# One-tile fp32 jobs for two experts after five units, a two-tile fp32 job after seven, and a written order through the ninth unit

## The chip, the core and the metric

One core of a Trainium2 chip runs the whole program. The metric is device time in microseconds, as the median of three runs. The engines are PE (TensorE, matmuls; its weight loads are PEld), DVE (VectorE), ACT (ScalarE), POOL (GpSimd) and SP (SyncE, which here only issues transfers).

## The reference

A gated scan over 4 sequences of 3648 steps with 256 channels, and then a mixture of 16 experts in 4 groups of 4, of which each token takes one.

```python
sig = 1.0 / (1.0 + np.exp(-f_logit))
f = lower_bound + (1.0 - lower_bound) * sig
for t in range(S):
    h = f[:, t] * h + (1.0 - f[:, t]) * x[:, t]
    y[:, t] = h
# x = y as 14592 tokens of 256
g_idx = argmax(x @ w_group); g_w = softmax(x @ w_group)[g_idx]
# for the tokens of group g
e_idx = argmax(xg @ w_expert[g]); e_w = softmax(xg @ w_expert[g])[e_idx]
h = np.maximum(xg @ w1[g, e], 0.0)      # 256 -> 1024
out = g_w * e_w * (h @ w2[g, e])        # 1024 -> 256
```

## The kernel before

Phase 1 goes through the tokens in 29 units of 512 (`UNIT`). For each unit a transfer brings gate and input (tile `zt`, 1 MB; p1_load, SP for units under 9, then ACT's queue, two units ahead). ACT makes tanh and affine (p1_tanh, p1_affine; together p1_ta), DVE the gated product and the scan of both halves of the channels (p1_gate, p1_tb), PE the routing logits (p1_router, p1_logits) and the transposes back to token rows (p1_back, tile `rows`). Every one or two units (GROUPS) a routing step on DVE and PE works out the place of each token in its expert's list (`posi`), and POOL scatters the rows, 128 at a time, into the lists `xs` in DRAM (s7).

Phase 2 is the experts. Each expert has an early job, kind A: EARLY gives for expert e the unit count after which the list is cut (first number), and how many tiles of 128 rows are taken from below the cut (second). close_early works out the place (`posA`), early_rows has SP read the rows (`xr`), and early_blanks writes blank rows ahead of the list, for a list that is still shorter. Sixteen jobs of kind B, longest first, then take what is left of each list; CAPS is the row count for which each of them is built, and a loop at the end would take what exceeds a cap.

A job has four pieces of weights, 512 KB each (job_weights), then its rows transposed (job_xt: `xh`, `xl`), a first layer (m1_step, banks of 512 columns, `hh`, `hl`) and a second one (m2_step, 8 matmuls of 256 columns and a row scale `o`, then POOL's scatter to the output). Ordinary jobs split weights, rows and hidden values into an fp16 high and a bf16 low part (job_split: a cast to `wh` on ACT, a subtraction to `wl` on DVE) and use three matmuls for a product. The first RAW jobs take fp32 as it is, with one matmul that runs in several passes, and `xh`, `xl`, `wh`, `wl`, `hh`, `hl` are then just halves of the channels.

Order: up to unit 8 the program gives PE, DVE and ACT their order as written (manual_schedule; p1_thunks with `u <= cut + 1`). Afterwards the steps of phase 1 are dealt out between the steps of the jobs at a rate (`due`, bg_step), and a scheduler may move an instruction of one engine ahead of others. Job 0 starts when `marks["begun"]` is reached. SP issues in the order written throughout:

```python
for u, n in EARLY_FETCH:
    while u not in last_load:
        bg_pop()
    fetch_to(n)
bg_to(first)
start_macro(0)
```

Of the kernel before, what the change touches and what calls it, by code (L numbers as in the profile page):

```python
# [24 lines left out]
CAPS = [848, 748, 724, 592, 588, 560, 528, 488, 464, 460, 448, 420, 392, 296, 168, 112]  # L25
# [3 lines left out]
EARLY_FETCH = [(5, 4), (8, 8)]  # L29
STG_BUFS = 8  # L30
RAW = 2
# [10 lines left out]
def gated_scan_moe(ctx: ExitStack, tc, zx, lower, wroute, wexp, out, S):  # L42
# [234 lines left out]
    def route_thunks(G, T, fast=False):  # L277
# [64 lines left out]
        def s7(t0, t1):  # L342
            for t in range(t0, t1):
# [43 lines left out]
    def p1_thunks(us, groups):  # L387
# [28 lines left out]
        cut = EARLY[0][0]  # L416
# [13 lines left out]
        for u in us + [us[-1] + 1]:  # L430
            seq = []
            if u <= cut + 1:
                put(lambda u=u: (p1_load(u + AHEAD - 1), early_blanks(u + 4)))
                ending = u - 1 in ends and u <= cut
# [7 lines left out]
                put(lambda u=u: p1_tb(u, 0))  # L442
                if ending:
# [5 lines left out]
                    if u > 1 and member[u - 2] == member[u - 1]:  # L449
                        put(lambda u=u: p1_back(u - 2, 0))  # L450
                        put(lambda u=u: p1_back(u - 2, 1))
# [4 lines left out]
                    put(lambda u=u: p1_back(u - 1, 0))  # L456
                    put(lambda u=u: p1_back(u - 1, 1))
# [5 lines left out]
                elif u > cut:  # L463
                    put(lambda u=u: p1_back(u - 1, 0))
                    put(lambda u=u: p1_back(u - 1, 1))
                if u == cut:
                    put(lambda u=u: close_early(u))
                    f = lambda u=u: early_rows(u)
                    f.mark = u
                    put(f)  # L470
                f = lambda u=u: p1_tb(u, 1)
                if u == cut + 1:
                    f.mark = "begun"
                put(f)
# [14 lines left out]
            for t in seq:  # L489
                put(t)  # L490
                slot += 1
                for _ in range(2 if u <= EARLY[0][0] else 1):
# [9 lines left out]
            if u - 1 in ends:  # L502
# [10 lines left out]
                if u in cuts and u > cut:  # L513
# [36 lines left out]

    def early_rows(u):
        for mac in macros:
# [5 lines left out]
    early_loads = []  # L558

# [551 lines left out]
```

## Time and profile before

| | |
|---|---|
| median of 3 runs (lowest, highest) | 815.78 us (814.15, 817.62) |
| profiled execution: time, span | 819.72 us, 818.0 us |
| PE busy | 732.8 us, 90% of the span |
| DVE, ACT, POOL busy | 525.2, 453.8, 284.3 us |
| PE share of the chain that ended last | 73% |
| mean DMA rate | 190 GB/s |

Busy time is the time in which an engine had an instruction in work. A row of the timeline has the start, the duration, the engine (a q behind it marks the issue of a transfer), line, operation, tiles written and read, and in brackets how long the engine had been idle and what released it. PE records an fp32 matmul twice.

### The profile page before, as it was taken

What the parts mean: (1) busy time and instruction counts of PE and PEld (TensorE: products, weight loads), DVE (VectorE), ACT (ScalarE), POOL (GpSimd) and SP (SyncE); (2) the same over time, 40 slices, a digit from 0 to 9 for tenths busy, and PEclk for the clock granted to TensorE, in tenths of its full rate; (3) what the DMA queues carried; (4) which work ended last, traced back from release to release, by engine and by line L of the source; (5) the groups of instructions that cost most, each with busy time, mean ns of one, the idle gap of its engine ahead of it and who ended that gap; (6) DMA issues with size and microseconds to landing.
All of it is one profiled execution on the core that took longest, in us unless ns stands there. A gap on an engine that the chain in (4) does not pass through costs nothing.

```text
span 818.0 us, 20715 instructions
## 1 busy us (share of the span) xinstructions
PE 732.8 (90%) x8048; PEld 640.5 (78%) x8048; DVE 525.2 (64%) x1040; ACT 453.8 (55%) x818; POOL 284.3 (35%) x272
## 2 busy tenths in 40 slices
PE   2644888999999898779999999999999999999996
PEld 1423667889788687569898898998988989889995
DVE  6755889899889776266555535545545656555650
ACT  6445487877677755235454445544544655556641
POOL 3662264477646352541112222212222222132222
PEclk9999989999999899999999999999999999999998
DMA  7997989999999645329553552543643555555400
GB/s 264 333 314 230 348 232 385 325 338 330 344 247 348 214 131 175 110 76 284 125 127 113 141 123 82 143 114 109 165 119 111 144 152 160 164 163 156 119 28 23
DMA packets 97156, 155.57 MB, mean 190 GB/s; under 512 B 52448, under 2 KB 64765, under 8 KB 93728
## 3 DMA queue, kind: packets, MB, share of 16 engines
q1 hardware_dynamic: 82080, 103.73, 43.9%
q0 software_dynamic: 11424, 30.02, 10.7%
q10 hardware_dynamic: 3552, 20.48, 6.8%
q8 instruction: 63, 1.03, 0.5%
q14 instruction: 37, 0.30, 0.1%
HBM read 112.69 MB, written 42.02 MB: 189 GB/s over the span
## 4 chain that ended last, share of the span: by engine, by line
PE 73%; issue 6%; DVE 5%; DMA 4%; ACT 1%; POOL 1%; POOLq 0%; DVEq 0%; SPq 0%; ACTq 0%
PE ps_m L894 35%; PE ps_m L871 8%; PE ps_m L873 8%; PE ps_m L872 7%; PE ps_p L872 3%; PE ps_p L871 3%; PE ps_p L873 3%; DMA zt<-in_zx_dram 3%; DVE wl L775 2%; PE ps_p L249 2%; PE ps_p L818 1%; PE ps_p L263 1%; PE ps_m L888 1%; PE ps_m L849 1%; POOL out_dram L907 1%
## 5 line engine op out<-in xcount | busy, mean ns | idle before, releaser
L894 PE MATMUL ps_m<-wl,hh 128*128 128x256 bf16 (+4 forms) x1288 | 259.9, 252 | 7.0 <-issue 6.9
L894 PE MATMUL ps_m<-wh,hl 128*128 128x256 f16 (+4 forms) x1288 | 259.6, 252 | 4.0 <-issue 4.0
L894 PE MATMUL ps_m<-wh,hh 128*128 128x256 f16 (+4 forms) x1288 | 259.9, 253 | 2.0 <-issue 1.7
L894 PEld LDWEIGHTS <-hh 128*128 128x128 f16 (+3 forms) x2576 | 191.0, 100 | 31.8 <-issue 11.7
L871 PE MATMUL ps_m<-xh,wh 128*128 128x256 f16 (+7 forms) x750 | 187.8, 260 | 7.6 <-issue 4.8
L872 PE MATMUL ps_m<-xl,wh 128*128 128x256 bf16 (+7 forms) x750 | 187.9, 260 | 2.0 <-DVE xl L828 1.4
L873 PE MATMUL ps_m<-xh,wl 128*128 128x256 f16 (+7 forms) x750 | 187.8, 260 | 1.2 <-issue 1.2
L775 DVE TENSOR_TENSOR wl<-st,wh 128x1024 bf16<-128x1024 f32 x120 | 144.9, 1218 | 64.5 <-ACT wh L774 62.9
L344 POOL DMA_INDIRECT xs<-rows,posi x114 | 133.4, 1170 | 135.1 <-DVE rows L326 49.3
L877 DVE SCALAR_TENSOR_TENSOR hl<-ps_m,hh 128x512 bf16<-128x512 f32 (+7 forms) x168 | 112.0, 669 | 92.4 <-issue 49.5
L907 POOL DMA_INDIRECT out_dram<-o,info x75 | 82.1, 1095 | 254.7 <-ACT o L906 210.5
L876 ACT ACTIVATE hh<-ps_m 128x512 f16<-128x512 f32 (+7 forms) x168 | 98.7, 589 | 91.1 <-PE ps_m L873 61.7
L774 ACT CAST wh<-st 128x1024 f16<-128x1024 f32 x120 | 124.3, 1049 | 11.7 <-PE ps_m L894 7.7
L894 PEld LDWEIGHTS <-hl 128*128 128x128 bf16 (+4 forms) x1288 | 102.1, 100 | 20.0 <-issue 9.9
L872 PEld LDWEIGHTS <-wh 128*128 128x128 f16 x1056 | 103.6, 98 | 17.8 <-issue 10.2
L873 PEld LDWEIGHTS <-wl 128*128 128x128 bf16 x1056 | 103.5, 98 | 12.5 <-issue 5.2
L871 PEld LDWEIGHTS <-wh 128*128 128x128 f16 x1056 | 103.8, 98 | 11.6 <-issue 3.6
L907 POOL DMA_INDIRECT out_dram<-o,meta x55 | 64.3, 1169 | 137.0 <-ACT o L906 120.6
L906 ACT ACTIVATE o<-ps_m,info 128x256 f32<-128x256 f32 (+4 forms) x75 | 33.1, 441 | 95.9 <-PE ps_m L894 86.4
L872 PE MATMUL ps_p<-xl,wh 128*128 128x256 bf16 (+13 forms) x306 | 73.5, 252 | 1.8 <-issue 1.8
L873 PE MATMUL ps_p<-xh,wl 128*128 128x256 f16 (+13 forms) x306 | 73.5, 252 | 0.5 <-issue 0.4
L871 PE MATMUL ps_p<-xh,wh 128*128 128x256 f16 (+13 forms) x306 | 73.7, 252 | 0.0
(165 smaller groups left out, 806.4 us busy)
## 6 DMA issues: line engine op xcount, KB each, us to landing
st<-in_wexp_dram SPq DMA_DIRECT2D x120, 512.0 KB
zt<-in_zx_dram ACTq DMA_DIRECT2D x19, 1024.0 KB
zt<-in_zx_dram SPq DMA_DIRECT2D x7, 1024.0 KB
xr<-xs SPq DMA_DIRECT2D x25, 258.0 KB
xs<-blank SPq DMA_DIRECT2D x22, 258.0 KB
wh<-in_wexp_dram SPq DMA_DIRECT2D x8, 256.0 KB
wl<-in_wexp_dram SPq DMA_DIRECT2D x8, 256.0 KB
xs<-rows,posi POOLq DMA_INDIRECT x114
```

The costliest lines, as they stand in the source:

```text
L249: nc.tensor.transpose(out=bp[:, (j - j0) * D + k * P:(j - j0) * D + (k + 1) * P], in_=h[:, k, j * P:(j + 1) * P], identity=ident)
L344: sc = nc.gpsimd.indirect_dma_start(out=xs_v[G["t0"] + t][:, :], out_offset=bass.IndirectOffsetOnAxis(ap=R["posi"][:, t:t + 1], axis=0), i ...
L774: nc.scalar.copy(j.wh[i], j.st[i])
L775: nc.vector.tensor_tensor(out=j.wl[i], in0=j.st[i], in1=j.wh[i], op=ALU.subtract)
L871: nc.tensor.matmul(po, w1_at(j.wh, k, c), xh[:, k], start=(k == 0), stop=False)
L872: nc.tensor.matmul(po, w1_at(j.wh, k, c), xl[:, k], start=False, stop=False)
L873: nc.tensor.matmul(po, w1_at(j.wl, k, c), xh[:, k], start=False, stop=(k == KD - 1))
L876: nc.scalar.activation(hi, pv, AF.Relu)
L877: nc.vector.scalar_tensor_tensor(out=j.hl[ch][:, cs[0]:cs[-1] + 1, 0:w], in0=pv, scalar=0.0, in1=hi, op0=ALU.max, op1=ALU.subtract)
L894: nc.tensor.matmul(pm[i * q:i * q + n, 0:dw], h[ch][:, c, ts], w2_at(w, c)[:, i * dw:(i + 1) * dw], start=(c == 0 and s == 0), stop=(c == ...
L906: nc.scalar.activation(o[s, 0:dw], pm[s, 0:dw], AF.Copy, scale=lt.bitcast(F32)[s, r, 1:2])
L907: nc.gpsimd.indirect_dma_start(out=out_v[out_n[0]].rearrange("n (g d) -> (n g) d", g=g), out_offset=bass.IndirectOffsetOnAxis(ap=lt[s, r, ...
```

## The change

EARLY: experts 0 and 1 are cut after five units with one tile (before: seven, two tiles); expert 2 after seven (before nine), expert 4 after nine (before eleven). CAPS grow to match. RAW goes from 2 to 3. The written order runs through unit 9 (FAST), and jobs 0 and 1 stand in it as parts that p1_thunks puts at the ninth unit (PLAN, first_parts, wave); their second layer is cut in two (raw2). Their rows are asked for at unit 8, those of job 2 at unit 9 (ROWS_AT). A read of early rows no longer waits for scatters of units behind its cut, nor a tail blank for any scatter. Weights are fetched up to 6 or 8 pieces ahead, but at most two at a time.

```diff
-EARLY = [(7, 2), (7, 2), (9, 2), (9, 2), (11, 2), (11, 2), (13, 3), (15, 3),
+EARLY = [(5, 1), (5, 1), (7, 2), (9, 2), (9, 2), (11, 2), (13, 3), (15, 3),
-CAPS = [848, 748, 724, 592, 588, 560, 528, 488, ...
+CAPS = [976, 812, 748, 616, 592, 588, 548, 488, ...
-EARLY_FETCH = [(5, 4), (8, 8)]
+EARLY_FETCH = [(5, 4), (8, 8), (-5, 12)]
+FAST = 9
+PLAN = [9, 9]
+ROWS_AT = {5: 8, 7: 9}
-RAW = 2
+RAW = 3
...
+                scatters.append(((G["t0"] + t) // (UNIT // P), sc.ins))
...
+        def wave(u, n):
+            while parts and n and parts[0][0] <= u:
+                put(parts.pop(0)[1])
+                n -= 1
...
-            if u <= cut + 1:
-                put(lambda u=u: (p1_load(u + AHEAD - 1), early_blanks(u + 4)))
-                ending = u - 1 in ends and u <= cut
+            if u <= FAST:
+                put(lambda u=u: (p1_load(u + AHEAD - 1), [early_blanks(v) for v in range(u + 4 if u else 0, u + 5)]))
+                for m in [m for m, v in ROWS_AT.items() if u == v]:
+                    f = lambda m=m: early_rows(m)
+                    f.mark = m
+                    put(f)
+                ending = u - 1 in ends
...
                 put(lambda u=u: p1_tb(u, 0))
+                wave(u, 1)
...
                     put(f4)
+                    wave(u, 1)
...
                     for f in s7s:
                         put(f)
+                    wave(u, 1)
...
+                put(lambda u=u: p1_tb(u, 1))
+                wave(u, 1 if u < FAST else 99)
...
     def tail_blank(s):
...
+        for _, sc in scatters:
+            tc.declare_no_dep(bl.ins, sc, reason="blank rows begin behind a list's last row")
...
                 early_loads.append(ld.ins)
+                for u, sc in scatters:
+                    if u >= EARLY[j.idx][0]:
+                        tc.declare_no_dep(ld.ins, sc, reason="rows scattered behind a cut lie above it")
...
+    def raw2(j, ch, t, cs, pm):
+        b, n, _ = j.parts[ch][t]
+        c0 = b - j.chunks[ch][0]
+        for c in cs:
+            nc.tensor.matmul(pm[0:n, 0:D], j.hh[ch][c // 4][:, c % 4, c0:c0 + n],
+                             (j.wh, j.wl)[c % 4 // 2][2 + c // 4][:, c % 2 * D:(c % 2 + 1) * D],
+                             start=(c == 0), stop=(c == KF - 1))
...
+    def first_parts():
+        out = []
+        for (j,), u in zip(macros, PLAN):
+            half = {}
+
+            def begin(j=j, half=half):
+                half[0] = bank("m2")
+                raw2(j, 0, 0, range(KF // 2), half[0])
+            fs = [lambda j=j: job_xt(j, 0)]
+            fs += [lambda j=j, cs=cs: m1_step(j, 0, cs) for cs in j.cols[0]]
+            fs += [begin, lambda j=j, half=half: m2_step(j, 0, 0, half[0])]
+            out += [(u, f) for f in fs]
+        return out
...
-            fetch_to(piece_index[(id(j), i)] + STG_BUFS)
+            at = piece_index[(id(j), i)]
+            fetch_to(max(at + 1, min(at + (6 if j.raw else STG_BUFS), pptr[0] + 2)))
...
         bg_to(marks["begun"])
-        for t in prep:
+        start_macro(len(PLAN))
+        for t in prep_thunks(macros[len(PLAN)][0]):
             t()
...
+        if mi < len(PLAN):
+            continue
```

What it moves, on two engines. ACT in the stretch in which units 8 and 9 are worked on, before: the tanh of unit 9 (L185), the transfer of unit 11 (L175), the affine of unit 9 (L195), the router copy (L266), the tanh of unit 10, the logits (L275), unit 10's affine between the row copies of unit 7 (L251), and job 0's rows (L824).

```order
L185 ACTIVATE zt<-zt 128x1024
L175 DMA zt<-in_zx_dram 128x2048
L195 ACTIVATE zt<-zt,mid,half 128x512 x2
L266 COPY rs<-ps_p 128x128
L185 ACTIVATE zt<-zt 128x1024
L275 COPY Lg<-ps_p 128x80
L195 ACTIVATE zt<-zt,mid,half 128x512
L251 COPY rows<-ps_p 128x2x256
L253 COPY rows<-tokno 128x4
L195 ACTIVATE zt<-zt,mid,half 128x512
L251 COPY rows<-ps_p 128x2x256
L824 COPY xh<-ps_p 128x256
```

The same place after, from the transfer of unit 11 on (lines are shifted: L178 is the transfer, L188 the tanh, L198 the affine, L856 a raw job's rows, L884 a raw job's hidden values).

```order
L178 DMA zt<-in_zx_dram 128x2048
L269 COPY rs<-ps_p 128x128
L178 DMA zt<-in_zx_dram 128x2048
L278 COPY Lg<-ps_p 128x80
L856 COPY xh<-ps_p 128x128
L856 COPY xl<-ps_p 128x128
L188 ACTIVATE zt<-zt 128x1024
L375 ACTIVATE ex<-ge 128x160
L188 ACTIVATE zt<-zt 128x1024 x2
L198 ACTIVATE zt<-zt,mid,half 128x512 x4
L884 ACTIVATE hh<-ps_m_914 128x4x128
L198 ACTIVATE zt<-zt,mid,half 128x512 x2
```

Job 0's rows now come before the tanh of unit 10, and the tanh of units 10, 11 and 12, the second transfer of the piece being unit 12's, stand ahead of job 0's first hidden values. Further down on ACT after, between job 0 and job 2:

```order
L806 CAST wh_1169<-st 128x1024
L178 DMA zt<-in_zx_dram 128x2048
L884 ACTIVATE hh<-ps_m_1019 128x4x128
L884 ACTIVATE hl<-ps_m_1029 128x4x128
L178 DMA zt<-in_zx_dram 128x2048
L188 ACTIVATE zt<-zt 128x1024
L945 ACTIVATE o<-ps_m_1039,meta 128x256
L856 COPY xh<-ps_p 128x256
L856 COPY xl<-ps_p 128x256
```

The transfers are those of units 13 and 14, the tanh that of unit 13; the rows of job 2 (L856, 256 columns) are behind it, and the cast ahead is the last of job 3's four. DVE before, from the end of unit 8 on:

```order
L231 SCALAR_TENSOR_TENSOR zt<-zt 128x1024
L222 SCALAR_TENSOR_TENSOR h<-zt,h 128x512 x2
L830 COPY meta<-xr 128x4
L211 SCALAR_TENSOR_TENSOR zt<-zt 128x1024
L222 SCALAR_TENSOR_TENSOR h<-zt,h 128x512 x2
```

DVE after, from the end of unit 9's routing on (L382 the places, L214 the gate, L566 and L568 posA, L225 the scans, L862 the copies from the rows of jobs 1 and 2, L807 the low half of job 3's weights):

```order
L382 TENSOR_REDUCE posi<-sc 128x8
L214 SCALAR_TENSOR_TENSOR zt<-zt 128x1024 x3
L566 SCALAR_TENSOR_TENSOR posA<-runoff,taken 128x2
L225 SCALAR_TENSOR_TENSOR h<-zt,h 128x512
L568 TENSOR_SCALAR taken<-posA 128x2
L225 SCALAR_TENSOR_TENSOR h<-zt,h 128x512
L862 COPY meta<-xr 128x2
L862 COPY meta<-xr 128x4
L807 TENSOR_TENSOR wl_1110<-st,wh_1109 128x1024
```

Before, the copy from job 0's rows stands ahead of unit 9; after, the gates of units 10, 11 and 12 stand ahead of posA and of unit 9's second scan.

More of the change, by code (lines that the diff above doesn't have):

```diff
@@ L415, in p1_thunks, with back @@
         put(lambda: p1_ta(us[0]))
-        cut = EARLY[0][0]
+        backed = set()
+        def back(v):
+            if v not in backed:
+                backed.add(v)
+                put(lambda v=v: p1_back(v, 0))
+                put(lambda v=v: p1_back(v, 1))
+        def wave(u, n):
+            while parts and n and parts[0][0] <= u:
+                put(parts.pop(0)[1])
+                n -= 1
         def routing(v):
@@ L462, in p1_thunks @@
                         put(f)
[L463 to L466, printed above, removed]
-                    put(lambda u=u: close_early(u))
-                    f = lambda u=u: early_rows(u)
-                    f.mark = u
+                    wave(u, 1)
+                elif u > 7:
+                    wave(u, 1)
+                    back(u - 1)
+                if u in cuts and u - 1 in ends:
+                    put(lambda u=u: close_early(u))
+                put(lambda u=u: p1_tb(u, 1))
+                wave(u, 1 if u < FAST else 99)
+                if u == FAST:
+                    f = lambda: None
+                    f.mark = "begun"
                     put(f)
[L471 to L474, printed above, removed]
+                    for v in [v for v in sorted(cuts) if v <= FAST and v not in ROWS_AT]:
+                        f = lambda v=v: early_rows(v)
+                        f.mark = v
+                        put(f)
                 continue
@@ L491, in p1_thunks @@
                 slot += 1
-                for _ in range(2 if u <= EARLY[0][0] else 1):
+                for _ in range(1):
                     if not hold:
@@ L512, in p1_thunks @@
                 put(bind)
-                if u in cuts and u > cut:
+                if u in cuts:
                     rs.append(lambda u=u: close_early(u))
@@ L549, in close_early @@
                     j.pos = posA
+    asked = set()
     def early_rows(u):
+        asked.add(-u)
         for mac in macros:
@@ L886, in m2_step @@
         ts = slice(c0, c0 + n)
-        for c in range(KF if j.raw else 0):
-            nc.tensor.matmul(pm[0:n, 0:D], j.hh[ch][c // 4][:, c % 4, ts],
-                             (j.wh, j.wl)[c % 4 // 2][2 + c // 4][:, c % 2 * D:(c % 2 + 1) * D],
-                             start=(c == 0), stop=(c == KF - 1))
+        if j.raw:
+            raw2(j, ch, t, range(KF // 2 if begun else 0, KF), pm)
         for c in range(0 if j.raw else KF):
@@ L991, in gated_scan_moe @@
                 due[-1] = (at - work(mac) // 2, marks["order"])
-    now = [0]
+    now = [sum(work(mac) for mac in macros[:len(PLAN)])]
     credit = [0.0]
@@ L1006, in bg_step @@
         now[0] += n
-    first = marks[EARLY[0][0]]
     with tc.manual_schedule(engines={mybir.EngineType.PE, mybir.EngineType.DVE, mybir.EngineType.Activation}):
         for u, n in EARLY_FETCH:
-            while u not in last_load:
+            while u not in last_load and u not in asked:
                 bg_pop()
             fetch_to(n)
-        bg_to(first)
-        start_macro(0)
-        prep = prep_thunks(macros[0][0])
         bg_to(marks["begun"])
-        for t in prep:
+        start_macro(len(PLAN))
+        for t in prep_thunks(macros[len(PLAN)][0]):
             t()
```

28 lines of the change are left out of this document (14 added, 14 removed).

## The prediction

> **What bounds the kernel now.** I read the busy times by stage first, then the chain of work that ended last, then each engine's rows in order of time over the first 130 us. Columns of the first fence: the stretch, its length, then busy us (and instructions) of PE, PEld, DVE, ACT and POOL, the granted clock, the DMA share and GB/s.
>
> ```profile
> 0.00:122.00 122.00, 70.80 (x500) 52.06 (x501) 85.01 (x196) 71.75 (x145) 54.28 (x71) 0.97 0.90 286
> 122.00:260.00 138.00, 132.16 (x1310) 114.53 (x1310) 128.79 (x240) 107.54 (x201) 79.52 (x63) 0.99 1.00 329
> 260.00:380.00 120.00, 105.49 (x952) 88.56 (x950) 76.79 (x188) 59.26 (x110) 48.80 (x46) 0.94 0.51 173
> 380.00:790.00 410.00, 404.30 (x4997) 366.93 (x4996) 229.40 (x410) 209.09 (x353) 95.92 (x88) 1.00 0.48 131
> ```
>
> From 122 us on PE is busy 132.2 of 138, 105.5 of 120 and 404.3 of 410 us, so a matmul taken out there is time saved, one added is time lost. Before 122 us PE is idle for 51.2 us, and no other engine is full either: that stretch is a chain of waits. What is in the chain:
>
> ```profile
> 70.02 5.64 DMA xs<-rows,posi
> 75.91 2.73 DMA xr<-xs
> 91.44 8.77 DMA zt<-in_zx_dram
> 239.38 13.44 DMA zt<-in_zx_dram
> 495.89 2.62 PE ps_m L894 x24
> 508.49 0.89 PE ps_m L894 x77
> ...
> 68.80 2.47 DVE L222 TENSOR_TENSOR_SCAN h<-zt,h 128x512 f32<-128x512 f32 x2
> 78.67 0.17 DVE L830 COPY meta<-xr 128x4 int32<-128x4 int32 x1 [7.40 <-DMA xr<-xs]
> ...
> 123.96 0.68 DVE L828 TENSOR_TENSOR xl<-ps_p,xh 128x512 bf16<-128x512 f32 x1
> 124.69 0.27 PE L872 MATMUL ps_m<-xl,wh 128*128 128x256 bf16 x1 [1.40 <-DVE xl L828]
> ```
>
> The scans of unit 8 end at 71.3. Then everything waits until 78.67: the last scatter of unit 6 takes 5.64 us to land, the read of job 0's rows 2.73 more, and DVE's next instruction copies from those rows. The other end of the early stage is 124.69, where PE takes the low half of the rows of job 2, the first job with split weights. I sum the change as the shift of that moment plus the PE work that then remains.
>
> **The change part by part: the PE work.** A full tile of a split job costs 24 matmuls of 256 columns in the second layer, 2.62 us, and as many column passes in the first (48 on 128 columns): 5.24 us. EARLY falls from 55 to 53 tiles and RAW rises from two jobs of two tiles to one, one and two, so four tiles stay fp32 and two split tiles go: -10.5 us. CAPS grow from 7836 to 8128 rows: 292/128 x 2.62 = 6.0 us in the first layer. By make_job's cutting the B jobs then have 59 full parts instead of 56, and 6 quarter parts instead of 8. A quarter part is 96 short matmuls at 0.89/77 us, 1.1 us. So the second layer gains 3 x 2.62 - 2 x 1.1 = 5.7 us, and the B jobs 11.7 in all. Counted from the reference's inputs, every list is still 8 to 11 rows under its cap, so the loop for leftovers stays empty. Nothing hides this: +1.2 us of PE in total.
>
> **The rows' wait.** Jobs 0 and 1 now need only units 0 to 4.
>
> ```profile
> 54.75 0.97 POOL L344 DMA_INDIRECT xs<-rows,posi  x1 [0.30 <-issue]
> 59.82 0.27 ACT L266 COPY rs<-ps_p 128x128 f32<-128x128 f32 x1 [6.01 <-remote]
> 70.06 1.91 PE L249 MATMUL ps_p<-ident,h 128*128 128x128 f32 x8
> 51.99 1.11 PE L263 MATMUL ps_p<-h,wr 128*32 128x128 f32 x16
> ```
>
> The row at 54.75 is the twentieth scatter, the last of unit 4. With 5.64 to land and 2.73 for the read the rows are there at 63, before anybody asks. The reading of job 2's rows (two tiles, after seven units) waits as today until 75.7 and is hidden behind jobs 0 and 1. So the 7.4 us stall goes. What is late next is the ACT queue, which the order of instructions shows: copies of unit 7, the transfer of unit 11, the router copy of unit 8, the transfer of unit 12, then, ahead of job 0's first hh, the tanh of units 10, 11 and 12. A tanh waits for its transfer, and behind it stand every affine, hh, hl, cast and xh up to job 2; DVE waits too, since its gates of units 10 to 12 stand ahead of posA and of unit 9's second scan.
>
> When is unit 12 asked for? PE ends the transposes of unit 7 at 71.97, the router takes 1.11, its copy 0.27: 73.4. The transfer of unit 12 is not in today's trace under these loads, so I bound it by transfers of the same size.
>
> ```profile
> 65.30 0.33 ACTq L175 DMA_DIRECT2D zt<-in_zx_dram  x1
> 71.20 1.06 ACT L185 ACTIVATE zt<-zt 128x1024 f32<-128x1024 f32 x1 [1.47 <-DMA zt<-in_zx_dram]
> ...
> 90.30 0.60 ACT L251 COPY rows<-ps_p 128x512 f32<-128x512 f32 x1
> 90.78 0.62 ACT L852 ACTIVATE hh<-ps_m 128x512 f32<-128x512 f32 x1
> 91.27 0.35 ACT L312 ACTIVATE ex<-ge 128x160 f32<-128x160 f32 x1
> ...
> 91.82 1.06 ACT L185 ACTIVATE zt<-zt 128x1024 f32<-128x1024 f32 x1
> 92.78 0.57 ACT L251 COPY rows<-ps_p 128x512 f32<-128x512 f32 x1
> 93.25 1.52 ACT L195 ACTIVATE zt<-zt,mid,half 128x512 f32<-128x512 f32 x2
> 94.67 0.19 ACT L253 COPY rows<-tokno 128x4 int32<-128x4 int32 x1
> 113.79 1.99 ACT L774 CAST wh<-st 128x1024 f16<-128x1024 f32 x2
> 79.92 0.37 ACT L824 COPY xh<-ps_p 128x256 f32<-128x256 f32 x1 [5.07 <-PE ps_p L818]
> ```
>
> Bounds: 5.9 us (65.30 to 71.20, little else moving) and 13.4. For unit 12 I take 8.8, since unit 11 and five pieces of 512 KB move with it. It lands at 82.2, its tanh ends at 83.2. Then, from start to start: three pairs of affines at 1.42, hh and hl at 0.49, two row copies at 0.48, four casts in two pairs of 1.99, and six short ones (two tokno, runoff, o, xh, xl) for some 1.3: 11.6 us, to 94.8, where unit 13 is asked for. There I take 5.9: SP then stands at the rows of jobs 3 and 4, which wait for unit 8's scatters, and asks for nothing. That gives 100.7, the tanh 0.96, o, xh and xl 1.1: job 2 starts on PE at 102.8.
>
> From there DVE carries the chain: unit 12's scan needs a buffer that PE frees after job 2's first bank and the second half of unit 9's transposes.
>
> ```profile
> 95.42 1.03 PE L888 MATMUL ps_m<-wh,hh 128*128 128x256 f32 x4
> 96.29 1.03 PE L888 MATMUL ps_m<-wl,hh 128*128 128x256 f32 x4
> 103.60 2.08 PE L888 MATMUL ps_m<-wh,hl 128*128 128x256 f32 x4 [4.69 <-ACT zt L185]
> 82.44 1.20 DVE L211 SCALAR_TENSOR_TENSOR zt<-zt 128x1024 f32<-128x1024 f32 x1
> 83.75 2.46 DVE L222 TENSOR_TENSOR_SCAN h<-zt,h 128x512 f32<-128x512 f32 x2
> 87.35 0.32 DVE L284 TENSOR_REDUCE mx<-Lg 128x40 f32<-128x160 f32 x1 [1.14 <-ACT Lg L275]
> 89.63 0.42 DVE L302 TENSOR_TENSOR_SCAN scn<-rmask,oh 128x128 bf16<-128x128 bf16 x1
> 114.87 2.36 DVE L775 TENSOR_TENSOR wl<-st,wh 128x1024 bf16<-128x1024 f32 x2 [0.92 <-ACT wh L774]
> ```
>
> Four fp32 records of 256 columns take 0.87 from start to start, two matmuls, so a bank of four is 1.74; with the transposes 2.2. Then on DVE two scans 2.4, a gate 1.2, two low halves of weights 2.4, two scans 2.4, the first seven routing steps 2.7 (87.35 to 90.05) and xl 0.68: 11.8. The low half of job 3's rows is ready at 116.8. Today's (job 2's) is ready at 124.6: the moment comes 7.8 us earlier.
>
> At both moments PE has one half of a two-tile fp32 job left (the same 6.9 us), but phase 1 is one unit further back in the new order: the transposes and the router of one unit, about 1.6 us more for PE. Sum: -7.8 - 10.5 + 11.7 + 1.6 = -5.0 us, where the split tiles' 10.5 stands for job 2's place being taken by job 3.
>
> The rest has one answer each. A one-tile fp32 job is 16 matmuls of 128 columns and 8 of 256; 128-column fp32 is not in the trace with such weights: between half of a 256-column one (6.9 us for the job) and the same (10.4); I take half, the rows being paced by columns. One job fewer is split: four casts and four subtractions leave ACT and DVE, which do not bound after 122 us; cost and gain nothing while PE is 96% busy there. The slower fetching (at most two pieces at once) puts fewer pieces ahead of the inputs; I give it nothing, 0 to 1 us either way. Two blanks of 132 KB go ahead of unit 4's transfer: at 329 GB/s 0 to 0.8 us, taken as 0, since unit 4's tanh is three units behind them. The waits declared away for the tail blanks lie behind two jobs of six tiles, 63 us of PE. The wider B jobs' masks: an eighth column.
>
> **Clock.** In the rows above, the four matmuls at 103.60 took 2.08 us after a wait of 4.69, those at 95.42 1.03. The Trainium skill, "TensorE: Matmul & The Clock Gate", section "HAM oscillation — how this bites in real kernels", says that waits longer than the activity window put the array back to half rate, again and again. The trace agrees by the doubled row; by that rule jobs 0 and 1, cut up by ACT's waits, run at half rate throughout, and the sum would be about 1 instead of -5. It is the third rival below.
>
> **Rivals.**
> - Slower: ACT is held longer at the two tanh. If both transfers took 13.4 us, as at 239.38, the chain is 4.6 + 7.5 = 12.1 us later: 822.6. The point at which it decides: the two together over 23.8 us instead of 14.7. For it: the DMA share of 0.90 over the first 122 us. Against it: that 13.4 is from the middle of the fullest stretch. "DMA: Bandwidth & Descriptors" of the Trainium skill, section "Issuing engines are not separate DMA queues", says that transfers of all issuers interleave on the same 16 engines; by it SP's five pieces lengthen unit 12's transfer, as the 8.8 already has it.
> - Faster: transfers are there in time (5.9 for both) and the 6.01 us for which ACT stood at 59.82, released by nothing that the profile names, does not come back: 810.8 - 2.9 - 6.0 = 801.9. For it: nothing in the code asks for that wait. Against: the rows up to there hardly change.
> - Given back: job 1 at half rate takes 6.9 us more, of which the wait for unit 13 covers under 1 (at full rate the job ends near 101, the tanh at 101.7): about 817. Against it: part of jobs 0 and 1 runs back to back.
> - Given back by transfers: at a DMA share of 1.00 from 122 to 260 us the transfers could set the pace, and job 2's saved 10.5 us would be idle: 815.8 - 7.8 + 11.7 = 819.7. Against it: PE idles for only 5.8 us of those 138.
>
> **How the numbers follow.** The profiled execution took 819.72 us around a span of 818.0; the median of the runs is 815.78. I take the difference off the median: 815.8 - 5.0 = 810.8, 0.6% down. Half a percent, 4.1 us, is about what a measurement of this kernel can tell from no change, so the forecast stands close to that edge. Chances: the forecast 0.42 (its own range 806 to 815, three quarters of it under 811.7), earlier transfers 0.18, the two ways of giving back 0.25, slower through the two tanh 0.15. Faster: 0.32 + 0.18 = 0.50 and a little of the rest, 0.51; slower 0.15; no change 0.34. Leaving out one in ten at each end gives 801 to 821.
>
> **What would show it.** Right: the 7.40 us before the meta copy gone; ACT idle before the tanh of unit 12 near 73 to 82 and of unit 13 near 95 to 101, put down to the input transfer; job 2's first fp32 matmuls near 103 and the first low-half matmul of a split job near 117; the B jobs 11 to 12 us longer, the split jobs before them 10 shorter. Wrong: waits of ACT for the inputs over 10 us each; PE's clock at half in both one-tile jobs with job 2 after 108; new PE waits between 122 and 260; or a list over its cap.

## The result, and the profile after

The kernel after takes 828.0 us (median of ten runs, 819.8 to 833.0), the kernel before, measured beside it, 815.6 (ten runs). The means, 826.2 and 816.3, are in the ratio 1.0121, with a 95% interval of 1.0083 to 1.0159; the run of 833.0 fell in a slower state and is left out of the mean. The forecast was 810.8. The profiled execution of the kernel after took 829.56 us around a span of 827.8.

The stretches of the kernel after, with the columns of the prediction's first fence (length, then busy us of PE, PEld, DVE, ACT and POOL, granted clock, DMA share, GB/s):

```profile
0.00:122.00 122.00, 72.65 (x545) 55.89 (x546) 83.59 (x192) 73.08 (x146) 47.60 (x66) 0.79 0.92 308
122.00:260.00 138.00, 120.54 (x1143) 99.40 (x1144) 115.12 (x218) 95.70 (x182) 75.92 (x63) 0.94 0.93 291
260.00:380.00 120.00, 108.95 (x1011) 93.75 (x1009) 83.40 (x202) 63.72 (x118) 53.20 (x48) 0.96 0.59 192
380.00:800.00 420.00, 415.94 (x4933) 378.53 (x4932) 233.06 (x409) 213.29 (x360) 98.34 (x89) 1.00 0.49 129
```

The second row is the one to read. Between 122 and 260 us PE was busy for 132.16 us before and for 120.54 after: it idles 17.5 us instead of 5.8. Some of that work only comes later (the third row has 108.95 where it was 105.49). What was won in all shows at the end of the early jobs. These are ACT's rows for the row scale of the last tile of the last early job, before and after:

```profile
473.30 0.47 ACT L906 ACTIVATE o<-ps_m,meta 128x256 f32<-128x256 f32 x1 [0.31 <-PE ps_m L894]
```

```profile
473.82 0.47 ACT L945 ACTIVATE o<-ps_m,meta 128x256 f32<-128x256 f32 x1 [0.31 <-PE ps_m L933]
```

The early jobs end at the same moment, 473.3 and 473.8, although the kernel after has two split tiles less in them (10.5 us by the prediction) and brings the rows of its first split job to PE 6.5 us earlier. From the start to that end, before and then after:

```profile
0.00:473.77 473.77, 402.22 (x3639) 339.69 (x3640) 342.69 (x712) 284.60 (x529) 201.16 (x196) 0.97 0.75 239
```

```profile
0.00:474.29 474.29, 396.42 (x3580) 334.04 (x3581) 334.60 (x700) 278.93 (x521) 195.98 (x194) 0.92 0.76 238
```

PE has worked 5.8 us less and DVE 8.1 us less, and both have idled the more. From there on only the B jobs follow, and those are longer.

What became of the removed wait is seen on DVE. In the order of time, the longest waits of DVE in the kernel after between 70 and 115 us:

```profile
76.81 0.32 DVE L287 TENSOR_REDUCE mx<-Lg 128x40 f32<-128x160 f32 x1 [6.01 <-ACT Lg L278]
...
87.24 1.22 DVE L214 SCALAR_TENSOR_TENSOR zt<-zt 128x1024 f32<-128x1024 f32 x1 [6.56 <-ACT zt L198]
...
106.78 2.46 DVE L225 TENSOR_TENSOR_SCAN h<-zt,h 128x512 f32<-128x512 f32 x2 [4.23 <-PE ps_p L252]
```

The 7.40 us at the copy from the rows are gone, and 6.01, 6.56 and 4.23 us stand in their place. The first is new to the prediction. It comes from ACT, which stood with the issue of unit 12's transfer in hand:

```profile
71.94 0.27 ACT L269 COPY rs<-ps_p 128x128 f32<-128x128 f32 x1 [3.00 <-DMA wh<-in_wexp_dram]
76.18 0.33 ACTq L178 DMA_DIRECT2D zt<-in_zx_dram  x1
76.55 0.23 ACT L278 COPY Lg<-ps_p 128x80 f32<-128x80 f32 x1 [4.35 <-DMA wl<-in_wexp_dram]
```

Around the two issues of input transfers (units 11 and 12) ACT was idle for 3.00 and 4.35 us, released by the landing of weight pieces that no instruction of ACT reads there. So the logits of unit 8, which stand behind the issue, came late, and with them DVE. The same two waits stand in later profiles of this order, 5.63 and 2.32 us in `e2_old_fetch`, 6.33 and 2.42 in `e9_after_again`; the profile of before has none of them. Columns as above, the first 115 us and the next 165, before and then after:

```profile
0.00:115.00 115.00, 64.60 (x456) 47.17 (x457) 78.15 (x187) 64.75 (x134) 48.50 (x67) 0.97 0.89 289
115.00:280.00 165.00, 155.46 (x1487) 132.12 (x1486) 150.03 (x271) 127.16 (x234) 96.12 (x77) 0.97 0.96 313
```

```profile
0.00:115.00 115.00, 66.42 (x473) 50.98 (x473) 77.63 (x170) 67.89 (x136) 47.60 (x66) 0.78 0.91 306
115.00:280.00 165.00, 146.77 (x1407) 122.18 (x1407) 138.62 (x274) 115.40 (x218) 88.66 (x74) 0.95 0.93 293
```

By 115 us DVE has worked 78.15 us before and 77.63 after: for DVE nothing began earlier. And phase 1 is further behind than it was: the tanh of unit 14, before and after.

```profile
107.51 1.07 ACT L185 ACTIVATE zt<-zt 128x1024 f32<-128x1024 f32 x1
```

```profile
116.02 1.06 ACT L188 ACTIVATE zt<-zt 128x1024 f32<-128x1024 f32 x1
...
138.16 1.06 ACT L188 ACTIVATE zt<-zt 128x1024 f32<-128x1024 f32 x1 [3.10 <-DMA zt<-in_zx_dram]
...
160.03 1.06 ACT L188 ACTIVATE zt<-zt 128x1024 f32<-128x1024 f32 x1 [4.89 <-DMA zt<-in_zx_dram]
```

Unit 14 is 8.5 us later. The rows at 138 and 160 (units 16 and 18) show ACT waiting for inputs, which it did not do there before. The largest group of PE's waits between 122 and 260 us is for DVE (us in total, times, longest):

```profile
PE ps_m L903 <- DVE hl L909: 5.1, 4, 2.4
```

Taken by what ended them, PE's waits there are 6.4 us for DVE (2.5 before), 6.4 for nothing that the profile names (2.7 before), 3.1 for ACT (0.9) and 1.0 for transfers (0.3). So DVE accounts for only part of PE's new idle time in this pair.

### The profile page after: what moved, and what is told of

It is laid out like the page before. It is cut to its first block, busy times and chain, and to the rows that moved or that the text cites. A ratio compares the mean times of both kernels' runs of the same rounds, so it can differ in the third digit from the quotient of the medians.

```text
span 827.8 us, 20400 instructions
## 1 busy us (share of the span) xinstructions
PE 737.9 (89%) x7917; PEld 645.8 (78%) x7917; DVE 520.2 (63%) x1028; ACT 451.7 (55%) x816; POOL 280.9 (34%) x271
## 3 DMA queue, kind: packets, MB, share of 16 engines
q0 software_dynamic: 11408, 30.02, 10.5%
## 4 chain that ended last, share of the span: by engine, by line
PE 70%; DMA 9%; issue 7%; DVE 7%; ACT 4%; POOL 1%; SPq 1%; POOLq 0%; another core or an unknown queue 0%; DVEq 0%; ACTq 0%
PE ps_m L933 33%; PE ps_m L903 8%; PE ps_m L904 7%; PE ps_m L905 7%; DMA zt<-in_zx_dram 6%; PE ps_p L903 3%; PE ps_p L904 3%; PE ps_p L905 3%; DVE wl L807 2%; DVE h L225 2%; PE ps_p L252 1%; DMA wh<-in_wexp_dram 1%; DMA wl<-in_wexp_dram 1%; ACT wh L806 1%; ACT zt L198 1%
## 5 line engine op out<-in xcount | busy, mean ns | idle before, releaser
L933 PEld LDWEIGHTS <-hh 128*128 128x128 f16 (+5 forms) x2464 | 190.9, 100 | 28.1 <-issue 8.2
L903 PE MATMUL ps_m<-xh,wh 128*128 128x256 f16 (+10 forms) x742 | 187.5, 262 | 13.7 <-DVE hl L909 8.2
L904 PE MATMUL ps_m<-xl,wh 128*128 128x256 bf16 (+10 forms) x742 | 187.4, 261 | 1.6 <-issue 1.6
L905 PE MATMUL ps_m<-xh,wl 128*128 128x256 f16 (+10 forms) x742 | 187.3, 261 | 0.6 <-issue 0.6
L807 DVE TENSOR_TENSOR wl<-st,wh 128x1024 bf16<-128x1024 f32 x116 | 140.1, 1217 | 56.9 <-ACT wh L806 55.3
L909 DVE SCALAR_TENSOR_TENSOR hl<-ps_m,hh 128x512 bf16<-128x512 f32 (+9 forms) x166 | 110.7, 670 | 88.0 <-ACT hh L908 54.0
L908 ACT ACTIVATE hh<-ps_m 128x512 f16<-128x512 f32 (+9 forms) x166 | 97.3, 588 | 90.1 <-PE ps_m L905 65.5
L945 ACT ACTIVATE o<-ps_m,info 128x256 f32<-128x256 f32 (+3 forms) x76 | 33.9, 445 | 99.1 <-PE ps_m L933 89.9
L909 DVE SCALAR_TENSOR_TENSOR hl<-ps_p,hh 128x512 bf16<-128x512 f32 (+9 forms) x69 | 44.6, 646 | 52.7 <-ACT hh L908 33.6
L904 PE MATMUL ps_p<-xl,wh 128*128 128x256 bf16 (+11 forms) x314 | 75.8, 252 | 1.0 <-issue 1.0
L905 PE MATMUL ps_p<-xh,wl 128*128 128x256 f16 (+11 forms) x314 | 75.8, 253 | 0.3 <-issue 0.3
```

The lines of the kernel that those rows point to most:

```text
L807: nc.vector.tensor_tensor(out=j.wl[i], in0=j.st[i], in1=j.wh[i], op=ALU.subtract)
L903: nc.tensor.matmul(po, w1_at(j.wh, k, c), xh[:, k], start=(k == 0), stop=False)
L904: nc.tensor.matmul(po, w1_at(j.wh, k, c), xl[:, k], start=False, stop=False)
L905: nc.tensor.matmul(po, w1_at(j.wl, k, c), xh[:, k], start=False, stop=(k == KD - 1))
L908: nc.scalar.activation(hi, pv, AF.Relu)
L909: nc.vector.scalar_tensor_tensor(out=j.hl[ch][:, cs[0]:cs[-1] + 1, 0:w], in0=pv, scalar=0.0, in1=hi, op0=ALU.max, op1=ALU.subtract)
```

## The experiments

The kernel before took 778 to 780 us in some measurements and 816 to 819 in others, here called the 780 level and the 816 level. So every ratio below is against the kernel before measured beside it, with its 95% interval. The chip alone does not make the level: the record gives chip 14 for the kernel before at 818.7 (`e5_dve_light_after` to `e8_cut6`) and later at 778.2 (`e13_scan_twice_after` to `e16_light_after_again`). The traces tell the levels apart. At the 816 level PE at times stands still between the matmuls of one tile, which else start 0.11 us apart, and the profile names nothing that it waits for ("issue"). From the profile of before:

```profile
337.61 0.27 PE L894 MATMUL ps_m<-wl,hh 128*128 128x256 bf16 x1
339.55 0.27 PE L894 MATMUL ps_m<-wh,hl 128*128 128x256 f16 x1 [1.67 <-issue]
340.26 0.27 PE L894 MATMUL ps_m<-wh,hh 128*128 128x256 f16 x1 [0.44 <-issue]
341.66 0.37 PE L894 MATMUL ps_m<-wl,hh 128*128 128x256 bf16 x1 [1.13 <-issue]
```

PE's waits marked "issue" add up to 29.6 us before and 19.2 after, and ACT's waits marked "remote", which name no releaser either, to 31.3 and 20.3. All ten profiles at the 816 level have both kinds. The ten at the 780 level have no "remote" waits of ACT, and no "issue" waits of PE in the first 500 us. What causes them stays open. The result above was taken at the 816 level.

The theories. Theory 1: the units' input transfers set the pace of phase 1, and PE idles behind it. Theory 2: the slower fetching holds back weights. Theory 3, formed when these had been tried: DVE sets the pace. Theory 4, the last: phase 1's steps are only dealt out too late.

### The B jobs' price, and the fetching

`e1_caps_only`, the kernel before with

```diff
-CAPS = [848, 748, 724, 592, 588, 560, 528, ...
+CAPS = [976, 812, 748, 616, 592, 588, 548, ...
```

> The kernel before with the wider CAPS of the kernel after and nothing else (EARLY, RAW and the order as before, so the B jobs compute more rows than the lists hold). It measures the term of 11.7 us by itself. Theory 1 (the B jobs' price was right; what failed is that the 10.5 us taken out of the split jobs between 122 and 260 us became idle time of PE, because there the units' input transfers and not PE set the pace): 815.6 + 11.7 = 827.3, between 825 and 829, a ratio of 1.0145. Rival (the price of the B jobs was set too low and is the whole loss): 832 or more. Rival (too high): 822 or less.

Measured 1.014 (1.012 to 1.0159): 10.9 us of 780.0. The prediction's 11.7 stands, and this price is about the whole loss of the kernel after (9.9 us by the means, 12.5 by the medians).

`e2_old_fetch`, the kernel after with

```diff
-            fetch_to(max(at + 1, min(at + (6 if j.raw else STG_BUFS), pptr[0] + 2)))
+            fetch_to(piece_index[(id(j), i)] + STG_BUFS)
```

> The kernel after with the weights fetched eight pieces ahead as in the kernel before, instead of two at a time and six ahead for an fp32 job. Theory 2 (the slower fetching holds back weights, and so PE, between 122 and 260 us): 828.0 falls by 5 to 12 us, to 816 to 823. Theory 1 (the pace is set by the units' inputs, which share the transfer engines with whatever weights are under way): no gain, 827 to 833, since the same bytes are only asked for earlier.

Measured 1.0128 (1.0108 to 1.0149) at the 780 level, against 1.0121 for the kernel after at the 816 level: nothing gained, theory 2 falls at this level. The kernel after itself was not timed unchanged at the 780 level, and `e2_old_fetch` stands for it there. `e1_caps_only` and `e2_old_fetch` were measured on one chip and are free of the unnamed waits, so their early stages can be set side by side, from the start to the end of the early jobs, `e1_caps_only` (whose early stage is that of before) and then `e2_old_fetch`:

```profile
0.00:439.34 439.34, 389.43 (x3639) 335.50 (x3640) 341.27 (x710) 285.23 (x529) 208.25 (x196) 0.97 0.80 258
```

```profile
0.00:438.52 438.52, 382.90 (x3580) 330.74 (x3581) 333.17 (x700) 277.88 (x521) 205.84 (x194) 0.98 0.79 257
```

Here too the early jobs end together, 439.3 and 438.5. PE has worked 6.5 us less and DVE 8.1 us less (a split job fewer), and each has idled about as much more. By 115 us DVE has worked 83.67 us in the one and 80.72 in the other, so here too nothing began earlier for DVE. Between 122 and 260 us PE waits 1.0 us for DVE in `e1_caps_only` and 5.3 in `e2_old_fetch`.

### Lighter transfers

`e3_light_after` and `e4_light_before`, each with

```diff
+        if j.kind == "A" and 3 <= j.idx <= 10:
+            sync.dma_start(out=st[:, 0:64], in_=wexp[bass.ds(e * P, P), i * 1024:i * 1024 + 64])
+            j.st[i] = st[:, None, 0:64].broadcast_to([P, 16, 64])
```

> The kernel after in which the early jobs of experts 3 to 10 load 64 of the 1024 columns of each weight piece and use them sixteen times over: 15 MB less to transfer, every instruction of PE, DVE and ACT as before (these jobs' outputs are therefore others). Theory 1 (transfers set the pace of the units between 122 and 260 us): ACT no longer waits for the inputs there (12 us of waits before), PE's idle time there falls from 17.5 to 8 us or less, and the time from 828.0 to 812 to 819. Rival (PE idles there for the order of its instructions or for its clock, whatever the transfers do): less than 4 us gained, 824 or more.

> The same lightening in the kernel before: the early jobs of experts 3 to 10 load 64 of the 1024 columns of each weight piece and use them sixteen times over. Theory 1: PE idles there for only 5.8 us between 122 and 260, so at most 3 to 6 us are gained, 810 to 813, and the kernel after loses most of its disadvantage against it: the gap falls from 12.5 us to between -5 and 4. Rival: both gain the same, and the gap stays between 9 and 15 us.

Measured 1.0093 (1.0072 to 1.0115) and 0.9965 (0.995 to 0.998). Each gains some 3 us (the kernel after against the 1.0128 of `e2_old_fetch`), and the gap between them stays at 10 us. From 115 to 280 us, the light kernel after:

```profile
115.00:280.00 165.00, 157.12 (x1600) 136.74 (x1599) 157.57 (x303) 130.29 (x246) 105.40 (x81) 0.99 0.77 242
```

The transfer engines now have room (share 0.77), PE still idles for 7.9 us, and DVE works 157.57 of 165. Theory 1 falls at this level. `e16_light_after_again` was to repeat it where the profile shows ACT waiting for inputs:

> The kernel after with 64 of the 1024 columns of each weight piece loaded in the early jobs of experts 3 to 10, again, on another chip, since on the first one the profile of the kernel after showed no waits of ACT for inputs to speak of. Theory 1 for a chip on which it shows them (12 us between 122 and 210): 4 to 9 us gained, ratio to the kernel before 1.002 to 1.009. Theories 3 and 4: 0 to 4 us as on the first chip, 1.008 to 1.014.

It measured 1.0098 (1.008 to 1.0116), but it stood at the 780 level again (before: 778.2). Whether transfers take part at the 816 level, as the rows at 138 and 160 suggest, stays open.

### Load on DVE

`e7_scan_twice` and, at the 780 level, `e14_scan_twice_again` for the kernel before, and `e13_scan_twice_after` for the kernel after:

```diff
+            if k == 1 and 12 <= u <= 27:
+                nc.vector.tensor_tensor_scan(out=h[:, k, c0 - a:c1 - a], data0=ff[:, k, c0 - a:c1 - a],
+                                             data1=uu[:, k, c0 - a:c1 - a], initial=init,
+                                             op0=ALU.mult, op1=ALU.subtract)
```

> The kernel before in which the scan of the second half of the channels is done twice, with the same result, in units 12 to 27: 16 scans of 1.23 us, 19.7 us, more on DVE. Theory 3 (DVE has 2 to 5 us to spare there): 13 to 18 us slower, ratio 1.016 to 1.024. What the prediction said (DVE does not bound after 122 us, PE does): at most 5 us slower, 1.006 or less.

> The same doubled scan in the kernel before, again, so that both stand on one chip: 1.0069 as before, between 1.003 and 1.012.

> The kernel after with the scan of the second half of the channels done twice in units 12 to 27, 19.7 us more on DVE, with the orders of PE, ACT and SP unchanged. DVE's load as the limit (theory 3): more is lost than the 5.6 us that the same edit cost the kernel before, 9 to 16 us, a ratio to the kernel before of 1.024 to 1.035. Transfers or the dealing as the limit: as much as in the kernel before or less, 2 to 6 us, 1.015 to 1.022.

Measured 1.0069 (1.0037 to 1.0101) at the 816 level; 1.0206 (1.0183 to 1.023) and 1.0323 (1.03 to 1.0345) at the 780 level. At the 816 level 19.7 us more cost 5.6. At the 780 level they cost the kernel before 16.0, and the kernel after, measured from the 1.0128 of `e2_old_fetch` (its orders on PE, DVE and ACT are those of after, its fetching is not), 15.2. Stretch 115 to 280, before and after with the doubled scan:

```profile
115.00:280.00 165.00, 152.79 (x1510) 132.46 (x1510) 163.65 (x289) 126.18 (x233) 101.03 (x77) 0.98 0.95 316
```

```profile
115.00:280.00 165.00, 148.27 (x1457) 127.33 (x1456) 161.21 (x299) 122.60 (x231) 97.55 (x75) 0.95 0.91 296
```

DVE is busy for 163.65 and 161.21 of 165 us, PE only for 152.79 and 148.27. So at this level DVE's load is on the path of both kernels, not of the kernel after alone as expected: a us of DVE costs 0.8, and PE, which the prediction took for the bound, waits. At the 816 level a us of DVE costs 0.3; DVE has idle time in that stretch (15 us before, 26 after, in the two profiles above), and added load is partly swallowed.

Less load was tried three ways. `e5_dve_light_after` and `e6_dve_light_before` make one low half of weights instead of four:

```diff
+        if j.kind == "A" and 3 <= j.idx <= 10 and i > 0:
+            j.wl[i] = j.wl[0]
```

> The kernel after in which the early jobs of experts 3 to 10 make the low half of the weights for the first of their four pieces only and use it for all four: 24 subtractions of 1.18 us, 28 us, less on DVE; everything else as before (these jobs' outputs are therefore slightly others). Theory 3, which takes the place of theory 1 (DVE, busy for 97% of the time from 122 to 280 us in both kernels, sets the moment at which phase 1 ends, so PE work taken out there is idle time): PE's waits for hl and for the rows of the next job between 125 and 260 go, 6 to 9 us are gained, and the ratio to the kernel before falls from 1.0121 to 1.001 to 1.004. Rival (the order of PE, in which units and jobs alternate, makes it wait whatever DVE's load is): less than 3 us, 1.008 or more.

> The same 28 us off DVE in the kernel before. Theory 3: PE is already busy for all but 1 or 2 us between 122 and 260, so it gains at most 0 to 3 us (ratio 0.996 to 1.000). If it gains as much as the kernel after does, DVE isn't what tells the two apart.

`e10_short_wl_after` and `e11_short_wl_before` make 256 of the 1024 columns of each:

```diff
+        n = 256 if j.kind == "A" and 3 <= j.idx <= 10 else 1024
+        nc.vector.tensor_tensor(out=j.wl[i][:, 0:n], in0=j.st[i][:, 0:n], in1=j.wh[i][:, 0:n], op=ALU.subtract)
```

> The kernel after in which the early jobs of experts 3 to 10 make only the first 256 of the 1024 columns of each low half of the weights, and use those for all columns (their outputs are therefore slightly others): 32 subtractions of 1.2 us become some 0.4 us, 26 us less on DVE, with the same instructions, waits and buffers everywhere. Theory 3 (phase 1's units come closer together after unit 12 than in the kernel before, so DVE has 18 scans in 122 to 195 us where it had 11, is full, and PE waits for it): PE's new idle time between 125 and 200 goes, 5 to 9 us, ratio to before 1.002 to 1.006. Rival (not DVE's load but the length of the chain of one unit through ACT, DVE and PE, with PE in order): 1.009 or more.

> The same 26 us off DVE in the kernel before. Theory 3: PE has little idle time to win there, 0 to 4 us, ratio 0.995 to 1.000. If it wins as much as the kernel after, DVE's load isn't what tells the two apart.

All four are slower: 1.0323 (1.0269 to 1.0376), 1.0298 (1.0255 to 1.034), 1.0204 (1.0159 to 1.025) and 1.0244 (1.0197 to 1.0292). They do not measure the load alone: in `e11_short_wl_before` the scheduler put 49 of DVE's 1040 instructions and 16 of PE's 8048 matmuls in other places. All four also stood at the 816 level, and ACT's "remote" waits between 122 and 260 us are 22.1, 21.2, 10.6 and 31.0 us in them, against 0.9 in the profile of before and 6.0 in that of after. From 115 to 280 us the engines of `e11_short_wl_before` read:

```profile
115.00:280.00 165.00, 144.26 (x1339) 119.76 (x1338) 111.42 (x250) 112.15 (x206) 69.65 (x66) 0.93 0.88 284
```

Against the profile of before, DVE works 39 us less, PE 11 us less as well, and nothing is full. Whether the changed order or the unnamed waits cost the time is not shown, so these four decide nothing about the load. `e17_weights_on_pool` keeps the orders of PE, ACT and SP and moves six small DVE instructions of each routing group to POOL:

```diff
+                W = nc.gpsimd
+                W.tensor_tensor(out=ex[:, :, :, 0:2], in0=ex[:, :, :, 0:2], in1=ex[:, :, :, 2:4], op=ALU.add)
+                W.tensor_tensor(out=sm, in0=ex[:, :, :, 0], in1=ex[:, :, :, 1], op=ALU.add)
...
+                    nc.gpsimd.tensor_tensor(out=rows[:, 0:n, D + 1], in0=s2_[:, at:at + n], in1=minus1[:, 0:n], op=ALU.pow)
```

> The kernel before in which, from unit 7 on, the softmax weights of a routing group (two sums, two products, the reciprocal: 6 DVE instructions, from start to start 0.9 us) are worked out on POOL, in seven to nine small instructions ahead of its scatters; the 1e-9 added in them is left out. The orders of PE, ACT and SP are unchanged, DVE has 66 instructions less, some 9 us between 105 and 280 us. Theory 3 (DVE's load sets the end of phase 1): where 19.7 us more cost 16.0, 9 us less bring 7, ratio 0.990 to 0.994; on a chip where they cost only 5.6, 2 to 3, 0.996 to 0.998. Rival (PE and DVE are both full, and a lighter DVE leaves PE as the limit, or the scatters start later for POOL's longer chain): 0.999 to 1.006.

Measured 1.0084 (1.0066 to 1.0103), the rival's side. POOL's rows of one group:

```profile
156.94 0.95 POOL L328 TENSOR_TENSOR ex<-ex 128x80 f32<-128x80 f32 x1
157.97 1.13 POOL L330 TENSOR_TENSOR sm<-ex 128x40 f32<-128x40 f32 x1
...
161.23 3.04 POOL L343 TENSOR_TENSOR rows<-s,minus 128x4 f32<-128x4 f32 x2
164.45 1.32 POOL L361 DMA_INDIRECT xs<-rows,posi  x1 [0.18 <-POOL rows L343]
```

From 156.94 to 164.45, 7.5 us go by before the group's first scatter, for about 1 us of DVE. "GPSIMD Engine Reference" of the Trainium skill, section "4.1 Engine selection", puts POOL at about half of DVE's speed for sums and products of two inputs; on some tiles this small the trace shows more (1.13 us for 128x40, where DVE takes 0.31 for the whole reduction that this sum is a part of). So that less load on DVE helps is not shown: every way of taking it off that was tried put something else in its place, and only the last was tried at the 780 level.

### Dealing, filling, and an earlier cut

`e15_dealt_earlier`, the kernel after with

```diff
-            credit[0] += rate * n
+            credit[0] += rate * n * (2 if now[0] < 28 else 1)
```

> The kernel after with phase 1's steps dealt at twice the rate during job 2: the transfers of units 13 and 14 go out earlier, their tanh, scans and transposes move ahead of some of job 2's and job 3's work. Theory 4 (phase 1 fell behind while jobs 0 to 2 held the order, and PE idles later while it catches up at a rate of 2.6 to 3.5 steps for one of PE's, where the kernel before has 1.5): unit 14's tanh, at 116 us in the kernel after, comes 4 us or more earlier, PE's idle time from 135 to 200 falls, 3 to 7 us are gained, ratio to the kernel before 1.004 to 1.011. Theory 3 (DVE has no time left from 100 us on, so earlier steps of phase 1 only put off its other work): less than 3 us either way, 1.010 to 1.018.

Measured 1.0267 (1.0242 to 1.0293), 11 us worse than `e2_old_fetch`, which also differs by its fetching. Its first two stretches, and the tanh of unit 14, which came only 0.4 us earlier than there:

```profile
0.00:115.00 115.00, 67.63 (x470) 50.93 (x470) 73.96 (x167) 66.57 (x134) 47.63 (x66) 0.96 0.91 315
115.00:280.00 165.00, 154.86 (x1547) 134.03 (x1546) 156.70 (x297) 130.02 (x247) 100.19 (x77) 0.99 0.94 311
```

```profile
111.61 1.06 ACT L188 ACTIVATE zt<-zt 128x1024 f32<-128x1024 f32 x1
```

Neither theory 4's gain nor theory 3's "little either way": DVE idled 7 us longer in the first stretch (73.96 of work by 115, where `e2_old_fetch` has 80.72), and the early jobs end 9 us later (447.0 against 438.1). Theory 4's gain did not come, but since unit 14 hardly moved, the edit did not do what the theory asks for, and it is not refuted.

`e9_after_again` and `e12_fill_after`, the latter the kernel after with

```diff
-EARLY = [(5, 1), (5, 1), (7, 2), (9, 2), (9, 2), (11, 2), ...
+EARLY = [(5, 1), (5, 1), (7, 2), (9, 3), (9, 2), (11, 3), ...
```

> The kernel after, unchanged, as the measure for the other kernels of this call, since chips differ: a ratio to the kernel before of 1.0121, as measured first, between 1.009 and 1.016.

> The kernel after with a third tile in the early jobs of experts 3 (after nine units) and 5 (after eleven): 10.5 us of PE and 3.4 us of DVE more where PE now idles, and CAPS 220 rows smaller, 8.7 us of PE less in the B jobs. Theory 3: about half of the 10.5 us fills idle time, since PE's share of the work rises against DVE's there: 3 to 6 us faster than the kernel after, ratio to before 1.005 to 1.009. Rival (that idle time can't be used, every tile costs its full price where it stands): 2 us slower than the kernel after, 1.013 to 1.016.

Measured 1.0157 (1.0103 to 1.0212) and 1.0114 (1.006 to 1.0169), medians 830.75 and 827.77. The intervals overlap, so the gain is not certain by the times; the last early tile's rows are plainer, the kernel after and then with two tiles more:

```profile
474.65 0.47 ACT L945 ACTIVATE o<-ps_m,meta 128x256 f32<-128x256 f32 x1 [0.31 <-PE ps_m L933]
```

```profile
476.05 0.47 ACT L944 ACTIVATE o<-ps_m,meta 128x256 f32<-128x256 f32 x1 [0.32 <-PE ps_m L932]
```

Two tiles, 10.5 us of PE by the prediction's price, end the early jobs only 1.4 us later, in one profile of each. This looks like the prediction's error turned round: PE work put into that stretch costs little, as PE work taken out of it brings little.

`e8_cut6`, the kernel before with the rows' wait removed (through the early jobs the engines keep their order, but for DVE's instructions on posA):

```diff
-EARLY = [(7, 2), (7, 2), (9, 2), ...
+EARLY = [(6, 2), (6, 2), (9, 2), ...
...
+                if u == cut:
+                    f = lambda: early_rows(6)
+                    f.mark = 6
+                    put(f)
```

> The kernel before with only the rows' wait taken away: experts 0 and 1 are cut after six units instead of seven (still two tiles, same order of the engines through unit 8), and their rows are asked for one unit after the cut, before unit 6's scatters; CAPS grow by 64 rows, 2.8 us of PE in the B jobs. The last scatter of unit 5 goes out at 59.86 in the profile of before; with 5.64 and 2.73 the rows are there at 68.2, before the scans of unit 8 end at 71.3. Theory 3: the 7.4 us in which DVE waits for the rows go, DVE and so phase 1 and every job shift by that: -7.4 + 2.8 = -4.6 us, a ratio of 0.994, between 0.991 and 0.998. Rival (DVE then waits for something else at the same place, the ACT queue or the inputs): 1.000 to 1.004.

Measured 0.9962 (0.9935 to 0.9988): 3.1 us faster, the one version with unchanged outputs that beats both kernels. DVE's rows at that place:

```profile
67.45 0.14 DVE L835 COPY meta<-xr 128x4 int32<-128x4 int32 x1
...
73.14 1.23 DVE L211 SCALAR_TENSOR_TENSOR zt<-zt 128x1024 f32<-128x1024 f32 x1 [1.85 <-ACT zt L195]
...
80.93 0.32 DVE L284 TENSOR_REDUCE mx<-Lg 128x40 f32<-128x160 f32 x1 [4.01 <-ACT Lg L275]
```

The copy no longer waits; 5.9 us of new waits stand behind it where there had been 7.40 and 1.14. `e18_cut6_weights_on_pool` has this edit and that of `e17_weights_on_pool`, both as shown above:

> The same together with the cut after six units (0.9962 by itself). If the two add up: 0.986 to 0.990 on a chip of the first kind, 0.992 to 0.995 on one of the second. If the earlier cut is worth less once DVE is lighter, or the other way round: no better than the better of the two.

Measured 1.0039 (1.0016 to 1.0061) where the edit on POOL alone has 1.0084: the earlier cut is worth 0.45% at the 780 level, where it was worth 0.38% at the 816 level.

## Why the prediction was wrong, step by step

- **The B jobs' price, 11.7 us: right.** 10.9 by `e1_caps_only`; in the profiles of before and after PE is busy for 10.9 us more after the early jobs (341.52 against 330.61).
- **The chain of the early replay: right as a chain.** Unit 13 was asked for at 94.43 (94.8 predicted), its tanh began at 100.33 (100.7), job 2's rows were copied at 103.40 (102.8), job 3's low half was ready at 118.1 (116.8). Only unit 12 was asked for later, at 76.18 instead of 73.4, for the wait on the weights' landing that no step had. That the later times fit in spite of it is partly luck: unit 12's tanh ended at 85.8 instead of 83.2, but unit 13 was asked for before the last cast ahead of it in ACT's order had begun (95.59), where the replay had waited for that cast's end.
- **The moment that was shifted: the wrong one.** The 7.8 us (6.5 measured) are a shift of PE. DVE, which has the scans of all later units, had worked as much by 115 us as before, and unit 14 came 8.5 us later. The prediction said that ACT and DVE "do not bound after 122 us", with PE 96% busy; its own first fence has DVE at 128.79 of 138 in the same row. The doubled scan shows what a full DVE means: a us on it costs 0.8 at the 780 level, and still 0.3 at the level at which that row was taken.
- **"-10.5 us" for the split tiles, as time saved: wrong.** "A matmul taken out there is time saved, one added is time lost" is the step that failed. PE's work in the early stage fell by 5.8 us (6.5 at the 780 level), and nothing of it was saved: the early jobs end at the same moment with and without those tiles at both levels (473.3 and 473.8, 438.9 and 438.1), and two more tiles cost 1.4 us instead of 10.5.
- **"Cost and gain nothing while PE is 96% busy there": right in the outcome, not in the reason.** The missing split job took 8.1 us off DVE and nothing was gained, but not because PE set the end: PE had less to do as well, and DVE idled 7.3 us more.
- **The rival "given back by transfers"** had the right place and sign, and was set aside on PE's 5.8 idle us, an average that says how long PE waits now, not how long it would wait with less to do. Its cause was only partly right: with 15 MB less to transfer (242 GB/s in that stretch instead of 311) the gap stays, at the 780 level. Its time, 819.7, kept the 7.8 us of shift; without them it is 827.5. (The first rival's 822.6 should read 822.9: 810.8 and 12.1.)
- **The faster rival's wait.** The 6.01 us at 59.82 are one of the "remote" waits above, which come at the 816 level and not at the 780 level, whatever the kernel. In the profile after, 2.29 us of it are left, and nothing was gained by that.
- **The clock rival fell.** The Trainium skill, "TensorE: Matmul & The Clock Gate", section "HAM oscillation — how this bites in real kernels", would have PE at half rate after long waits, and the profile after does grant 0.78 over the first 115 us. The second profile of the same kernel grants 0.99 there:

```profile
0.00:115.00 115.00, 68.93 (x481) 52.59 (x485) 77.98 (x171) 68.09 (x137) 48.47 (x66) 0.99 0.90 308
```

  and its early jobs end at 474.65 instead of 473.82: the granted clock in that stretch does not set the end. The rows agree with the rule once. After PE had waited 5.00 us, job 0's first bank ran at half pace, 0.43 us from pair to pair of records; job 1, which the rival priced at half rate, ran at 0.22:

```profile
80.53 0.63 PE L881 MATMUL ps_m<-xh,wh 128*128 128x128 f32 x2
80.96 0.64 PE L881 MATMUL ps_m<-xl,wh 128*128 128x128 f32 x2
...
96.16 0.39 PE L881 MATMUL ps_m<-xh,wh 128*128 128x128 f32 x2
96.38 0.39 PE L881 MATMUL ps_m<-xl,wh 128*128 128x128 f32 x2
```

The sum that fits: nothing for the earlier start, nothing for the tiles, 10.9 us (11.4 at the 816 level) for the B jobs, from 815.6 to 827.0; measured 828.0. Shown are the B price, the equal end of the early jobs, and that more load on DVE lengthens both kernels at the 780 level. That DVE is why the saved PE work came back as idle time is argued from this and not shown. Not settled are the shares of the input transfers and of the unnamed waits at the 816 level, and why lightening DVE in three ways never paid.

## What to carry to other kernels

Before a saving on the busiest engine is counted, look at the second busiest in the same stretch: here, with PE at 96% and DVE at 93%, work taken off PE came back as idle time. Count a removed wait on each engine that waited, not on the one where the path happened to pass, and look for the next wait in that engine's queue. Work moved out of a stage with two full engines into a stage with one is paid there in full.

## What was unexpected in the hardware

- Around the issue of two transfers ACT's queue stood for 3.00 and 4.35 us until, by the profile, unrelated weights had landed, and ACT's instructions behind the issues stood with it.
- The same kernel takes 778 to 780 us in some measurements and 816 to 819 in others, on the same chip number too. Its early jobs end at 473.3 us at the 816 level and at 438.9 at the 780 level (in `e1_caps_only`, whose early stage is the same), so nearly all of the difference lies before the B jobs. In the early jobs, PE stops between the matmuls of one tile at the 816 level alone, 1.67 us in the rows shown, with no cause in the profile.
- A small POOL sum of 128x40 took 1.13 us, and two powers over 128x4 together 3.04 us.
